# A fused attention and two-layer MLP kernel: the split of layer 2's input goes to GpSimd, one weight conversion for all, other orders at the start and the end

## The chip, the cores and the metric

One Trainium2 chip, one core. The metric is the device time of one execution in microseconds (us). The kernel before was run three times: 1339.81, 1341.20 and 1343.64 us, median 1341.2 us.

## The reference, cut to what matters

```python
# q (1,12288,128), kv (1,384,32,128), w_sr (128,128): float32; the four MLP weights come as float64
kv_pool = kv.reshape(B, H // 4, 4, W // 4, 4, C).mean(axis=(2, 4))     # 12288 rows -> 768 keys
k = v = kv_pool.reshape(B, -1, C) @ w_sr
a = softmax(q @ k.T / sqrt(128));  x = a @ v                            # 12288 x 128
h = x @ w_in;   x2 = (h * clip(h + 3, 0, 6) / 6) @ w_out                # layer 1, 128 -> 2048 -> 128
h = x2 @ w_in2; g = where(h >= 1, h, where(h <= -1, 0, (h + 1)**2 / 4))
out = g @ w_out2                                                        # layer 2, 128 -> 2048 -> 128
```

## The kernel before, in words

The 12288 queries are worked on in 24 blocks of 512. All products are made from two 16-bit parts of each factor, a high part (the value rounded) and a low part (the value minus the high part): three matmuls stand for one. So every activation is split before TensorE can use it: ScalarE rounds (`x_hi` L681, `cast` L785, `a_hi` L652), and VectorE or GpSimd subtracts (`x_lo` L687, `a_lo` L657, `low` L791, the last on GpSimd).

**Slots.** A block has 8 slots; slot T does 256 of the 2048 inner columns of layer 1 for pair s = T, and of layer 2 for pair s = T - 11 (`O2` L21). There are 192 pairs and 11 slots more at the end, in which layer 2 runs alone. In a slot TensorE does two times three matmuls of `m_in` (L695) and six of `m_out` (L710) for each layer. Attention of a later block is spread over the slots: four score tiles (`s`, `n`, `e`, `t`, `u`, `w`), two products with the values (`v`), the transpose of the queries (`q`, with its split in `i` and `j`).

**Orders written by hand.** `PROLOGUE` (L28) is the order of everything before slot 0: maxima of the weights (`m`), pooling of the keys (`k`, `g`, `t`), their product with w_sr (`p`, `z`, `y`), conversion of weights (`j`), attention of block 0, the first queries of block 1. Then `slot(T)` (L890) walks through one list of steps in each slot: `RAMP` (L38) in the slots before `RAMP_T` = 22, `SLOT` (L40) from there on. `name:g` means that the step is done g slots late. Each engine runs its instructions in the order in which these lists issue them. `LOADS` (L26) is the order of the input DMAs; a load is issued when one of 16 staging buffers has come free. They go through SyncE's queue, as do the transposes of the attention weights (L663) and the output DMAs (L741).

**Layer 2's input.** When layer 1 of a block is complete, its sum lies in a PSUM bank. `x2_max` (D, L490, VectorE) takes the largest magnitude in each partition, `x2_copy` (R, L496, ScalarE) copies the bank to SBUF, `x2_sum` (P, L499, TensorE) adds over partitions, `x2_scales` (F, L506 to L511, VectorE) makes a power of two of it and eight scalars, `x2_hi` (G, L516, ScalarE) and `x2_lo` (H, L521, VectorE) split. The first matmul of layer 2 for the block (step A0) needs both parts. F stands in slot 1 of the eight (counted from the block's end), G and H in slot 2, A0 in slot 3. The query transpose `q` stands in slot 2 as well.

**Weights.** They arrive as float64 and are turned into float32 bits with integer operations. For layer 1's input weight (4 tiles) this takes four stages (`w_stage0` to `w_stage3`, L291 to L336) on ScalarE, VectorE and GpSimd; for the other 12 tiles three (`w_new0`, `w_new1`, `w_stage3`). The largest magnitude of the first goes over GpSimd (`w_top_pool`, L208), of the other three over TensorE (`w_top_row`, `w_top_all`, L215 to L221). Seven tiles are converted in the prologue, nine in the slots of `CONV_AT` (steps B0, B1, B2).

**Keys.** Each of the 12 key tiles is pooled in one of three modes (`KV_MODE` L27): P, 16 matmuls into 32 of the partitions, then a copy and a TensorE transpose per pair of tiles; D, 16 matmuls with the tile as the weights, which need no transpose; V, two additions on VectorE and a few matmuls.

**The end.** Layer 2's sum of a block lies in the bank `acc1` until `o_T` (T, L734) has transposed it; `o_scale` (U, L739, ScalarE) scales it, four DMAs store it. The next block's first `m_out` of layer 2 waits for that bank.

Of the kernel before, what the change touches and what calls it, by code (L numbers as in the profile page):

```python
# [19 lines left out]
W_MIN = 3.4332275390625e-05  # L20
# [39 lines left out]
def tile_attn_moe_moe2(  # L60
# [70 lines left out]
    def new_h():  # L131
        return ps_h.tile([128, 512], FP32, tag="h", name="h")
# [18 lines left out]
    late = [0 if f"j{n}.{2 + (n % 2 == 0)}" in PROLOGUE.split() else 1 for n in range(len(late))]  # L151
# [55 lines left out]
    def w_top_pool(n):
        nc.gpsimd.partition_all_reduce(mw[n][:, 1:2], mw[n][:, 0:1], channels=128,  # L208
                                       reduce_op=bass_isa.ReduceOp.max)
        w_tops[n] = mw[n][:, 1:2]  # L210
# [13 lines left out]


    def w_scales(n):
        sc, u, v = w_sc[n], w_sc[n].bitcast(U32), mw[n].bitcast(U32)
        nc.vector.tensor_scalar(out=mw[n][:, 0:1], in0=w_tops[n], scalar1=2.0 ** -14, scalar2=None,
                                op0=ALU.max)
        nc.vector.tensor_scalar(out=v[:, 2:3], in0=v[:, 0:1], scalar1=0x7F800000, scalar2=None,  # L230
                                op0=ALU.bitwise_and)
# [59 lines left out]
    def w_stage0(job):  # L291
        t = wst[job][0]
        m, which, i = job
        half = W_DT[m] == FP16
        sc = w_sc[2 * m + (which == "out")]
        a = wk_p.tile([128, WP], U32, tag="wa", name="wa")
        r = wk_p.tile([128, WP], I32, tag="wr", name="wr")
        nc.scalar.activation(out=a.bitcast(FP32), in_=t[:, :, 1].bitcast(FP32), func=ACTF.Abs,
                             scale=sc[:, 0:1] if half else 1.0)
        low = t.rearrange("p a b -> p (a b)").bitcast(U8).rearrange("p (a b) -> p a b", b=8)  # L300
        if half:
            nc.scalar.activation(out=r.bitcast(FP32), in_=low[:, :, 3], func=ACTF.Identity,
                                 scale=sc[:, 2:3], bias=sc[:, 1:2])
        else:
            nc.scalar.activation(
                out=r, in_=low[:, :, 3], func=ACTF.Copy, scale=1.0 / 32.0, bias=1.0 / 64.0
            )
        wcv[job] = (a, r)

    def w_stage1(job):  # L310
        a, r = wcv[job]
# [4 lines left out]
        nc.gpsimd.tensor_tensor(out=a.bitcast(I32), in0=a.bitcast(I32), in1=r, op=ALU.add)

    def w_stage2(job):
        a, r = wcv.pop(job)
        hi32 = wst[job][0][:, :, 1]  # L320
        keep = 0x80000000 if W_DT[job[0]] == FP16 else 0xC0000000
        nc.vector.scalar_tensor_tensor(out=hi32, in0=hi32, scalar=keep, in1=a,
                                       op0=ALU.bitwise_and, op1=ALU.bitwise_or)

    def w_stage3(job):
# [7 lines left out]
        (nc.gpsimd.tensor_copy if w_new(job) and job not in LO_DVE else nc.scalar.copy)(out=hi[:, sl], in_=w)  # L333
# [39 lines left out]
    def kv_pool(i):  # L373
        m, mode = i // 2, KV_MODE[i]
        t = kv_t[i][0]
# [5 lines left out]
        for g in range(2):  # L381
# [9 lines left out]
        if mode == "P" and i % 2 == 1:  # L391
            nc.scalar.copy(out=pk[:, m * 128:(m + 1) * 128], in_=ps[:, :128])
# [597 lines left out]
```

## Time and profile before

| | |
|---|---|
| runs of the kernel before | 1339.81, 1341.20, 1343.64 us; median 1341.2 |
| the profiled execution | 1342.52 us; its span, first to last instruction, 1340.7 us |
| busy share of the span | TensorE 93%, VectorE 89%, ScalarE 86%, GpSimd 70% |
| chain that ended last | TensorE 59%, VectorE 20%, ScalarE 11% |

PE is TensorE's matmuls, PEld its weight loads, DVE VectorE, ACT ScalarE, POOL GpSimd, SP SyncE. Matmuls are pipelined: one of 512 columns is shown with 379 ns, while the next starts some 216 ns after it. "Idle before" is the time in which an engine did nothing just before an instruction, and "<-" names what ended it, inferred from semaphore events.

### The profile page before, as it was taken

The numbers are of one execution on the slowest core, as the hardware profiler recorded it, in microseconds if no ns is written. First come the engines' busy times: TensorE is split into PE (matmuls) and PEld (weight loads), VectorE is DVE, ScalarE is ACT, GpSimd is POOL, SyncE is SP. The second block draws the span as 40 slices with busy tenths as digits, with TensorE's granted clock in tenths as the row PEclk, the third lists the DMA queues.
The fourth block names the chain that finished last, engine by engine and source line by source line (L and its number), as shares of the span: only waits on it lengthen the run. The fifth ranks groups of instructions, "written<-read, shape, count | busy, mean of one in ns | idle before, by whom it ended". The sixth has DMA issues, their size and how long they took to land.

```text
span 1340.7 us, 19138 instructions
## 1 busy us (share of the span) xinstructions
PE 1247.0 (93%) x6280; PEld 662.2 (49%) x6280; DVE 1187.5 (89%) x1944; ACT 1158.6 (86%) x2028; POOL 941.9 (70%) x825
## 2 busy tenths in 40 slices
PE   7466789999999999999999999999999999999996
PEld 6333445455455555555455555555555555555442
DVE  4676799999999999999999999999999999999887
ACT  3465788998999998999998998899999999999986
POOL 2244687777777777777777777777777777777874
PEclk9687899999999999999999999999999999999998
DMA  8821113222222212222122122222122121121000
GB/s 301 219 44 36 32 26 50 44 39 45 39 37 53 40 35 52 36 40 52 32 44 52 33 44 49 33 46 47 36 45 44 37 48 36 32 45 32 1 9 17
DMA packets 260788, 66.32 MB, mean 49 GB/s; under 512 B 252368, under 2 KB 256592, under 8 KB 260688
## 3 DMA queue, kind: packets, MB, share of 16 engines
q1 hardware_dynamic: 257888, 63.73, 23.8%
q10 hardware_dynamic: 2800, 1.38, 0.4%
q8 instruction: 49, 0.80, 0.2%
q14 instruction: 51, 0.42, 0.1%
HBM read 21.04 MB, written 6.29 MB: 20 GB/s over the span
## 4 chain that ended last, share of the span: by engine, by line
PE 59%; DVE 20%; ACT 11%; issue 1%; DVEq 0%; ACTq 0%
PE h L707 24%; PE acc L725 23%; PE s L673 6%; PE s L593 5%; DVE g L777 5%; ACT h L785 4%; DVE g L764 3%; ACT t L749 2%; DVE t L756 2%; DVE x2l L521 2%; DVE bs L511 2%; ACT g L772 2%; ACT a L652 2%; DVE nm L604 2%; DVE bs L510 1%
## 5 line engine op out<-in xcount | busy, mean ns | idle before, releaser
L791 POOL TENSOR_TENSOR l<-g,h 128x512 f16<-128x512 f32 x382 | 450.1, 1196 | 274.7 <-DVE a L657 135.0
L791 POOL TENSOR_TENSOR l<-t,h 128x512 f16<-128x512 f32 x382 | 438.6, 1170 | 42.2 <-ACT h L785 39.2
L764 DVE TENSOR_SCALAR g<-h,bs 128x512 f32<-128x512 f32 x384 | 292.7, 804 | 23.7 <-PE h L707 23.6
L756 DVE SCALAR_TENSOR_TENSOR t<-t,h 128x512 f32<-128x512 f32 x384 | 255.8, 682 | 29.1 <-ACT t L749 25.9
L777 DVE SCALAR_TENSOR_TENSOR g<-g,bs,h 128x512 f32<-128x512 f32 x384 | 267.9, 737 | 14.0 <-ACT g L772 13.2
L785 ACT CAST h<-g 128x512 f16<-128x512 f32 x384 | 235.1, 615 | 42.2 <-PE acc L725 40.2
L749 ACT ACTIVATE t<-h,h_sc 128x512 f32<-128x512 f32 x384 | 252.5, 676 | 21.1 <-PE h L707 21.0
L772 ACT ACTIVATE g<-g,bs 128x512 f32<-128x512 f32 x384 | 259.7, 717 | 6.8 <-DVE g L764 3.6
L785 ACT CAST h<-t 128x512 f16<-128x512 f32 x384 | 235.6, 618 | 22.6 <-DVE t L756 21.2
L707 PE MATMUL h<-x2h,wi1h 128*128 128x512 f16 x384 | 145.6, 379 | 16.8 <-DVE g L777 16.8
L707 PE MATMUL h<-xh,wi0h 128*128 128x512 f16 x384 | 146.8, 382 | 10.2 <-ACT xh L681 6.2
L725 PE MATMUL acc<-h,wo1h 128*128 128x512 f16 x384 | 146.0, 380 | 3.9 <-DVE o L734 3.8
L725 PE MATMUL acc<-l,wo1h 128*128 128x512 f16 x384 | 145.9, 380 | 1.5 <-POOL l L791 1.5
L725 PE MATMUL acc<-h,wo0h 128*128 128x512 f16 x384 | 146.5, 381 | 0.8 <-DVE bs L506 0.8
L725 PE MATMUL acc<-l,wo0h 128*128 128x512 f16 x384 | 146.3, 381 | 0.5 <-DVE l L791 0.5
L725 PE MATMUL acc<-h,wo0l 128*128 128x512 f16 x384 | 146.1, 380 | 0.0
L725 PE MATMUL acc<-h,wo1l 128*128 128x512 f16 x384 | 146.0, 380 | 0.0
L707 PE MATMUL h<-xl,wi0h 128*128 128x512 f16 x384 | 145.9, 380 | 0.1
L707 PE MATMUL h<-xh,wi0l 128*128 128x512 f16 x384 | 146.0, 380 | 0.0
L707 PE MATMUL h<-x2h,wi1l 128*128 128x512 f16 x384 | 145.7, 379 | 0.0
L707 PE MATMUL h<-x2l,wi1h 128*128 128x512 f16 x384 | 145.5, 379 | 0.0
L707 PEld LDWEIGHTS <-wi1h 128*128 128x128 f16 x768 | 75.1, 98 | 113.9 <-issue 26.9
(183 smaller groups left out, 1843.6 us busy)
## 6 DMA issues: line engine op xcount, KB each, us to landing
out_dram<-o SPq DMA_DIRECT2D x96, 64.0 KB, 1.9
q<-in_q_dram SPq DMA_DIRECT2D x92, 64.0 KB, 2.3
wst<-in_kv_dram SPq DMA_DIRECT2D x9, 512.0 KB, 7.5
wst<-in_moe_w_in_dram SPq DMA_DIRECT2D x6, 512.0 KB, 6.2
wst<-in_moe_w_out_dram SPq DMA_DIRECT2D x5, 512.0 KB, 4.8
at<-a SPq DMA_TRANSPOSE x96, 3.7
g<-in_moe_w_out_dram SPq DMA_DIRECT2D x2, 512.0 KB, 7.9
g<-in_moe_w_in_dram SPq DMA_DIRECT2D x1, 512.0 KB, 4.2
```

What stands on the lines that cost most here:

```text
L511: nc.vector.tensor_scalar(out=t[:, 8:10], in0=b_k[:, 3:5], scalar1=t[:, 3:4], scalar2=None, op0=ALU.mult)
L593: nc.tensor.matmul(ps[h], l[:, js], r[:, ks], start=(n == 0), stop=(n == 2))
L673: nc.tensor.matmul(ps, l[:, k, :], r[:, k, :], start=(n == 0), stop=(n == 3 * KC - 1))
L707: nc.tensor.matmul(ps, l[:, ws], r, start=(n == 0), stop=(n == 2))
L725: nc.tensor.matmul(acc[m], l[:, ws], r[:, k, :], start=(c == 0 and i == 0), stop=(c == NPAIR - 1 and i == 5))
L749: nc.scalar.activation(out=g_t[0, s][:, k], in_=h_t[0, s, k], func=ACTF.Relu, scale=h_sc, bias=0.5 * H_SC)
L756: nc.vector.scalar_tensor_tensor(out=g, in0=g, scalar=H_SC, in1=h_t.pop((0, s, k)), op0=ALU.min, op1=ALU.mult)
L764: nc.vector.tensor_scalar(out=g_t[1, s][:, k], in0=h_t[1, s, k], scalar1=bs_t[s // NPAIR][:, 6:7], scalar2=bs_t[s // NPAIR][:, 7:8], op0=A ...
L772: nc.scalar.activation(out=g, in_=g, func=ACTF.Square, scale=bs_t[s // NPAIR][:, 8:9], bias=0.5)
L777: nc.vector.scalar_tensor_tensor(out=g, in0=g, scalar=bs_t[s // NPAIR][:, 6:7], in1=h_t.pop((1, s, k)), op0=ALU.mult, op1=ALU.max)
L785: nc.scalar.copy(out=hl_t[m, s][0][:, k], in_=g_t[m, s][:, k])
L791: eng.tensor_tensor(out=lo[:, k], in0=g_t[m, s][:, k], in1=hi[:, k], op=ALU.subtract)
```

## The change

- `x2_scales` keeps three instructions on VectorE; the two that make eight scalars go to GpSimd, into `x2_hi`. `x2_hi` scales the copy in place on GpSimd, `x2_lo` casts and subtracts on GpSimd. Five GpSimd instructions a block stand for three of VectorE and ScalarE.
- `q_hi` goes from ScalarE to GpSimd for blocks 2 and later, `o_scale` from ScalarE to GpSimd (VectorE in the last block).
- All 16 weight tiles are converted by the three stages. Layer 1's input weight has a power-of-two scale of its own for that (`x_scale`), taken into `x_sc`. Its largest magnitude goes over TensorE (`it`, `ib`).
- The V mode of the keys isn't used; P alternates between the two groups of a tile.
- `PROLOGUE`, `LOADS`, `RAMP` and `SLOT` are new orders, `RAMP` ends at slot 18, and the slots from 192 on have an order of their own, `TAIL`.
- In the last 11 slots every second pair of layer 2 takes score banks and layer 1's buffers, and the last block's layer 2 sums in `acc0`.

```diff
-LOADS = "w k0 k1 q0 w w w k2 k4 k3 k6 k5 k8 k7 k9 k10 k11 w w w w q1 w w w w w q2 w w w"
-KV_MODE = "DDVVPPPPPPPP"
+LOADS = "w k1 k3 k0 k2 w w w k4 k6 w k5 k7 w k8 k9 q0 k10 w w q1 k11 w w w w w q2 w w w"
+KV_MODE = "PPDDPPPPPPDD"
 PROLOGUE = """
...
-N3 e3 a2 b1 vs a3 vh b2 b3 vl m5 m7 oa ot q1 ob oc hs j1.0 x0 j1.1 j3.0 x1 j3.1 j1.2 j5.0 j3.2
-j5.1 j5.2
+k1 k2 g1 m0 m6 m4 m2 ia g3 it ib ic g2 g4 j2.0 k6 k4 j0.0 j2.1 k5 k3 g0 g5 k0 t1 p1 t2 g7 k7 p2 z1
...
+N2 vs n3 b0 e2 a2 N3 a1 oa e3 b2 ot vh b1 ob a3 q1 oc j5.0 b3 vl j1.0 j5.1 j1.1 j5.2 j3.0 j3.1 x0 x1
+j3.2 hs j1.2
 """
-RAMP_T = 22
-RAMP = """a0:0 r0:0 a1:0 r1:0 t:1 u:1 m0:0 m1:0 D:1 R:1 G:2 H:2 x:0 A0:0 K0:0 A1:0 K1:0 C0:1 L0:1 C1:1 L1:1 c0:0 l0:0 c1:0 l1:0
-T:3 U:3 Q0:0 Q1:0 s:0 n:0 w:1 P:1 F:1 X0:0 X1:0 e:0 v:0 z:0 y:0 q:0 i:0 j:0 B1:1 B2:2 B0:0 f o:1 O:2"""
+RAMP_T = 18
+RAMP = """
+a0 l0:1 j:2 q:1 L1:2 r0 a1 o:2 X1:1 x e:1 r1 f:1 y:1 O:3 m0 A0 G:2 A1 B0:1 l1:1 T:3 H:2 R:1 U:4 s D:1
+P:1 t:1 C0:1 m1 K0 K1 v F:1 C1:1 n c0 Q0 B1:1 L0:1 u:1 B2:3 z c1 X0 w:1 i:1 Q1
+"""
 SLOT = """
-a0 r0 B2:3 o:2 a1 l1:1 u:1 O:3 G:2 r1 y:1 D:1 B0:2 C0:1 R:1 m0 A0 A1 v w:1 c0 H:2 C1:1 j:1 m1 c1 K0
-K1 Q0 P:1 T:3 L0:1 s n q F:1 Q1 B1:3 L1:1 X0 e X1 f:1 t U:3 i z l0
+a0 L1:2 X1:1 t:1 r0 u:1 l0:1 o:2 z:1 a1 D:1 O:3 r1 A0 A1 q l1:1 G:2 y:1 v m0 w:1 C0:1 m1 R:1 T:3 i
+C1:1 c0 K0 K1 P:1 f:1 s j:1 U:3 c1 Q0 n B0:2 Q1 F:1 L0:1 H:2 B2:2 X0 B1:4 e
 """
+TAIL = """
+B2:3 n:1 P:2 L0:2 Q1:1 F:2 a0 B0:3 c0 m1:1 o:2 a1 O:3 D:1 c1 w:1 l0:1 s e r1 z:1 L1:2 v A0 t:1 T:3
+R:1 X0:1 G:2 i q j:1 l1:1 u:1 B1:4 X1:1 y:1 K0 C0:1 C1:1 r0 m0 A1 K1 U:3 H:2 Q0 f:1
+"""
+TAIL_T = 192
...
 def x2_scales(b):
...
-        nc.vector.tensor_scalar(out=t[:, 5:8], in0=b_k[:, 0:3], scalar1=t[:, 4:5], scalar2=None, op0=ALU.mult)
-        nc.vector.tensor_scalar(out=t[:, 8:10], in0=b_k[:, 3:5], scalar1=t[:, 3:4], scalar2=None, op0=ALU.mult)
 def x2_hi(b):
...
-        nc.scalar.activation(out=x2_t[b][0], in_=xr_t[b], func=ACTF.Copy, scale=bs_t[b][:, 5:6])
+        nc.gpsimd.tensor_scalar(out=t[:, 5:8], in0=b_k[:, 0:3], scalar1=t[:, 4:5], scalar2=None, op0=ALU.mult)
+        nc.gpsimd.tensor_scalar(out=t[:, 8:10], in0=b_k[:, 3:5], scalar1=t[:, 3:4], scalar2=None, op0=ALU.mult)
+        nc.gpsimd.tensor_scalar(out=xr, in0=xr, scalar1=t[:, 5:6], scalar2=None, op0=ALU.mult)
 def x2_lo(b):
...
-        nc.vector.scalar_tensor_tensor(
-            out=lo, in0=xr_t.pop(b), scalar=bs_t[b][:, 5:6], in1=hi, op0=ALU.mult, op1=ALU.subtract
-        )
+        xr = xr_t.pop(b)
+        nc.gpsimd.tensor_copy(out=hi, in_=xr)
+        nc.gpsimd.tensor_tensor(out=lo, in0=xr, in1=hi, op=ALU.subtract)
 def q_hi(b):
...
-        nc.scalar.copy(out=hi, in_=t)
+        (nc.gpsimd.tensor_copy if b > 1 else nc.scalar.copy)(out=hi, in_=t)
 def o_scale(b):
...
-        nc.scalar.activation(out=o, in_=o, func=ACTF.Copy, scale=bs_t[b][:, 9:10])
+        (nc.vector if b == NB - 1 else nc.gpsimd).tensor_scalar(out=o, in0=o, scalar1=bs_t[b][:, 9:10], scalar2=None, op0=ALU.mult)
...
+def spare(s):
+        return s > NS - O2 and (NS - s) % 2 == 0
 def m_in(m, s, k):
...
+        if m and spare(s):
+            if k == 0:
+                tail_s[s] = new_s()
+            ps = tail_s[s][:, k]
+        else:
+            ps = new_h()
 def m_out(m, s):
...
-            acc[m] = ps_a.tile([128, BLK], FP32, tag=f"acc{m}", name=f"acc{m}")
+            bank = "acc0" if b == NB - 1 else f"acc{m}"
+            acc[m] = ps_a.tile([128, BLK], FP32, tag=bank, name=bank)
```

## Rows read from the trace of the kernel before

**Rows 1.** Stages of core 0: length, busy us of each engine (instructions), granted clock, DMA share, GB/s.

```profile
0.00:71.45 71.45, 43.29 (x280) 34.70 (x280) 41.29 (x105) 28.00 (x58) 17.78 (x21) 0.86 0.80 244
71.45:203.10 131.65, 92.58 (x433) 51.12 (x434) 103.74 (x183) 92.21 (x161) 78.66 (x69) 0.88 0.21 37
203.10:290.50 87.40, 85.42 (x429) 44.56 (x428) 80.24 (x127) 80.98 (x143) 65.44 (x57) 1.00 0.27 44
290.50:1201.60 911.10, 900.70 (x4556) 473.78 (x4554) 843.93 (x1351) 843.00 (x1478) 681.21 (x595) 1.00 0.23 42
...
1291.50:1340.70 49.20, 35.51 (x152) 14.84 (x150) 39.35 (x58) 32.81 (x50) 25.97 (x22) 0.93 0.07 11
```

**Rows 2.** TensorE's waits, 290.5 to 1201.6 us: total, times, longest.

```profile
PE h L707 <- DVE g L777: 9.2, 27, 0.5
```

**Rows 3.** Timeline of VectorE: start, duration; `x2_max` of three blocks in a row.

```profile
1056.78 0.67 DVE L490 TENSOR_REDUCE mb<-acc 128x1 bf16<-128x512 f32 x1
...
1106.90 0.67 DVE L490 TENSOR_REDUCE mb<-acc 128x1 bf16<-128x512 f32 x1
...
1158.02 0.67 DVE L490 TENSOR_REDUCE mb<-acc 128x1 bf16<-128x512 f32 x1
```

**Rows 4.** The chain in order of time, pieces on `x2_lo`: start, us.

```profile
306.46 1.73 DVE x2l L521
...
1116.26 1.73 DVE x2l L521
```

**Rows 5.** Instructions on the tiles bs and x2l: min/median/max ns, first and last start.

```profile
L510 DVE TENSOR_SCALAR bs<-b_k,bs x24: 478/764/942, 139.9 to 1299.7; 128x3 f32<-128x3 f32 x24
L511 DVE TENSOR_SCALAR bs<-b_k,bs x24: 215/1198/1203, 140.7 to 1300.1; 128x2 f32<-128x2 f32 x24
...
L521 DVE SCALAR_TENSOR_TENSOR x2l<-xr,bs,x2h x24: 736/744/1733, 148.1 to 1301.5; 128x512 f16<-128x512 f32 x24
```

**Rows 6.** Groups by form, 290.5 to 1201.6 us: busy, mean ns, idle before, releasers.

```profile
L657 DVE SCALAR_TENSOR_TENSOR a<-e,rc,a 128x768 f16<-128x768 f32 x72 | 73.2, 1017 | 17.7 <-ACT a L652 15.8 <-DMA q<-in_q_dram 1.9
...
L516 ACT ACTIVATE x2h<-xr,bs 128x512 f16<-128x512 f32 x18 | 13.0, 725 | 0.0
...
L565 ACT CAST qh<-qT 128x512 fp32r<-128x512 f32 x18 | 10.9, 607 | 0.0
...
L791 POOL TENSOR_TENSOR l<-g,h 128x512 f16<-128x512 f32 x288 | 337.0, 1188 | 217.4 <-DVE a L657 124.5 <-ACT h L785 88.1 <-DVE t L756 2.5
```

**Rows 7.** Casts and subtractions of weight tiles on GpSimd (L333, L336): min/median/max ns.

```profile
L333 POOL CAST wo0h<-t x1: 634/634/634, 66.4 to 66.4; 128x512 f16<-128x512 f32 x1
L333 POOL CAST wo0h<-g x1: 1035/1035/1035, 69.3 to 69.3; 128x512 f16<-128x512 f32 x1
...
L336 POOL TENSOR_TENSOR wo0l<-t,wo0h x1: 1500/1500/1500, 67.2 to 67.2; 128x512 f16<-128x512 f32 x1
```

**Rows 8.** Timeline of one block: F's third instruction, and A0's first matmul.

```profile
605.91 0.17 DVE L509 RECIPROCAL bs<-bs 128x1 f32<-128x1 f32 x1
...
615.46 0.38 PE L707 MATMUL h<-x2h,wi1h 128*128 128x512 f16 x1
```

**Rows 9.** Timelines of TensorE and ScalarE, 0 to 80 us; in brackets the idle time before.

```profile
7.27 3.59 PE L387 MATMUL h<-pool_m,g 128*128 128x32 f32 x16 [7.27 <-DMA g<-in_kv_dram]
...
32.12 2.46 PE L385 MATMUL h<-wst,pool_m 128*32 128x128 f32 x32
...
60.43 0.61 PE L673 MATMUL h<-at,vh 128*128 128x256 f16 x2
...
70.90 0.65 ACT L333 CAST wo0h<-g 128x512 f16<-128x512 f32 x1 [3.12 <-DVE g L288]
71.45 1.26 ACT L749 ACTIVATE t<-h,h_sc 128x512 f32<-128x512 f32 x2
```

**Rows 10.** Timelines of TensorE and VectorE at the end.

```profile
1313.32 0.61 PE L725 MATMUL acc<-h,wo1h 128*128 128x512 f16 x1 [3.79 <-DVE o L734]
...
1317.08 1.53 DVE L764 TENSOR_SCALAR g<-h,bs 128x512 f32<-128x512 f32 x2 [2.52 <-PE h L707]
```

More of the change, by code (lines that the diff above doesn't have):

```diff
@@ L150, in tile_attn_moe_moe2 @@
     late = [0] * sum(f"j{j}.0" in PROLOGUE.split() for j in range(16))
-    late = [0 if f"j{n}.{2 + (n % 2 == 0)}" in PROLOGUE.split() else 1 for n in range(len(late))]
+    late = [0 if f"j{n}.2" in PROLOGUE.split() else 1 for n in range(len(late))]
     late += [1 if t + 3 < O2 else 2 for t in CONV_AT]
@@ L204, in w_top @@
     def w_top(n):
+        step("top", n)
+        for i in range(4):
+            assert ("max", (n, i)) in did
         nc.vector.tensor_reduce(out=mw[n][:, 0:1], in_=mw[n], axis=AX.X, op=ALU.max)
[L207 to L210, printed above, removed]
     def w_top_row(n):
-        step("row", n)
+        step("row", n, "top")
         w_tops[n] = new_h()
@@ L332, in w_stage3 @@
         sl = slice(i * WP, (i + 1) * WP)
-        (nc.gpsimd.tensor_copy if w_new(job) and job not in LO_DVE else nc.scalar.copy)(out=hi[:, sl], in_=w)
+        (nc.gpsimd.tensor_copy if job not in LO_DVE else nc.scalar.copy)(out=hi[:, sl], in_=w)
         eng = nc.vector if job in LO_DVE else nc.gpsimd
@@ L380, in kv_pool @@
         ps = pool_ps(m)
-        for g in range(2):
-            p0 = (2 * (i % 2) + g) * 32
+        if mode == "P":
             for j in range(4):
-                if mode == "P":
+                for g in range(2):
+                    p0 = (2 * (i % 2) + g) * 32
                     nc.tensor.matmul(ps[p0:p0 + 32, :128], pool_m, t[:, g, j], start=(j == 0), stop=(j == 3))
-                else:
+        else:
+            for g in range(2):
+                p0 = (2 * (i % 2) + g) * 32
+                for j in range(4):
                     nc.tensor.matmul(
@@ L390, in kv_pool @@
         died(kv_t[i][1])
-        if mode == "P" and i % 2 == 1:
+        if mode == "P" and ("k", i ^ 1) in did:
             nc.scalar.copy(out=pk[:, m * 128:(m + 1) * 128], in_=ps[:, :128])
     def kv_sum_mm(i):
+        if KV_MODE[i] != "V":
+            return
         t, rec = kv_t[i]
+        step("g", i, "k")
         ps = pool_ps(i // 2)
@@ L402, in kv_poolT @@
     def kv_poolT(m):
+        for i in (2 * m, 2 * m + 1):
+            assert ("g" if KV_MODE[i] == "V" else "k", i) in did
         ms = slice(m * 128, (m + 1) * 128)
@@ L428, in v_scale @@
     def v_scale():
+        for m in range(KC):
+            assert ("y", m) in did
         nc.vector.tensor_reduce(out=mx[:, 0:1], in_=mx, axis=AX.X, op=ALU.max)
@@ L680, in x_hi @@
         hi, lo = (t[:, i * 256:(i + 1) * 256] for t in x_t[b])
-        nc.scalar.activation(out=hi, in_=x_ps[b, i], func=ACTF.Copy, scale=2.0 ** -13)
+        nc.scalar.activation(out=hi, in_=x_ps[b, i], func=ACTF.Copy, scale=x_sc)
     def x_lo(b, i):
@@ L885, in tile_attn_moe_moe2 @@
     early_of = {bi: T < O2 for T, bi in av_at.items()}
[L886 removed]
+    orders = [[(n, int(g or 0)) for n, _, g in (t.partition(":") for t in o.split())] for o in (RAMP, SLOT, TAIL)]
     served = {}
     def slot(T):
[L891 removed]
+        for n, g in orders[(T >= RAMP_T) + (T >= TAIL_T)]:
             at, f = ops[n]
```

111 lines of the change are left out of this document (36 added, 75 removed).

## The prediction

> **What bounds the kernel now.** I read first the stages [rows 1]; they begin at the first ReLU of slots 0, 18, 32 and 176, and the last of them some 4 us after slot 191's ReLU. The middle, 290.5 to 1201.6, is 18 blocks in 911.10 us, 50.62 a block, and holds two thirds of the time. There TensorE is busy 900.70 us, so 10.4 us are left to win from waits alone. VectorE (843.93) and ScalarE (843.00) are at 93% each, GpSimd (681.21) at 75%. Second, TensorE's waits in that stretch [rows 2]: 9.2 us of its 10.4 idle us end with VectorE's `max2`, which gives back a PSUM bank of layer 2. Third, where VectorE is late: `x2_max` comes once a block, and the blocks have two lengths, 50.12 and 51.12 us [rows 3]. The chain of waits shows a piece of 1.73 us on `x2_lo` in each long block [rows 4]: nine in the 18 blocks, of which the first and the last are shown, and the last, at 1116.26, lies in the long block of [rows 3]. In the others this instruction takes its median of 0.74 us [rows 5]. One us late on VectorE at this place is one us of the block. The two small instructions before it behave likewise, 1.20 us for 128x2 elements where the shortest takes 0.215 [rows 5]. At the end GpSimd idles, where 1.20 was the rule and 0.215 the exception; so I read all three as VectorE held up while GpSimd works on SBUF.
>
> The other losses are outside the middle. Slots 0 to 17 take 131.65 us, 7.31 a slot, the next 14 take 87.40, or 6.24. In the former no engine is full: VectorE 103.74 of 131.65 (79%), ScalarE 92.21, TensorE 92.58 at a granted clock of 0.88. The last 49.20 us have VectorE at 39.35, TensorE at 35.51.
>
> **The change, part by part.**
>
> *VectorE and ScalarE in a block.* VectorE loses 0.76 + 1.20 + 0.74 or 1.73 [rows 5], on average 3.2 of its 46.9 us a block (843.93 / 18). ScalarE loses 0.725 (`x2_hi`), 0.607 (`q_hi`) [rows 6] and `o_scale`, which has the shape of `x2_hi` and which I put at the same 0.7: 2.0 of 46.8. Both were beside TensorE's work, so the removed time as such is worth nothing; worth something is the lateness. With `x2_lo` gone from VectorE the long blocks should become short: 9 x 1.00 = 9.0 us. If all of TensorE's idle time goes, it is 10.4. Below, nothing is won if another wait takes its place. I take 10, because VectorE also loses the two small instructions right before it. What would be late next is TensorE's own sequence.
>
> *GpSimd in a block.* Added are seven instructions. Casts on GpSimd took 0.634 to 1.035 us [rows 7], subtractions 1.188 on average [rows 6] to 1.50 [rows 7]. A multiplication by a scalar isn't in the trace; it lies between a cast (one input) and the slowest subtraction (two), 0.63 to 1.50, and I take 0.8, near the cast, since it reads one tensor. The two small ones have no row on GpSimd; VectorE's give 0.2 to 1.2 each, and I take 0.4. So the split costs 0.8 + 0.8 + 0.63 + 1.19 = 3.4 us (2.9 to 6.4), and with the queries' cast (0.63) and the output's scale (0.8) GpSimd goes from 37.8 (681.21 / 18) to 42.7 us a block, 47 at the upper ends. That is under 50.1, so it isn't a bound; and 217.4 us of idle time stand in front of its subtractions [rows 6], 12 a block, which hide it.
>
> The Trainium skill (GPSIMD Engine Reference, section 4.1) speaks against this move: elementwise work belongs on VectorE, GpSimd being about twice as slow with two inputs. The rows agree in direction (1.188 on GpSimd, 0.74 on VectorE), and by that rule the split would lose; it doesn't look at which engine has time left.
>
> *The path of the split.* F's third instruction ends at 605.91 + 0.17 = 606.08, A0's first matmul of the block starts at 615.46 [rows 8]: 9.38 us. GpSimd has in this stretch at most the four subtractions of a slot (4 x 1.19 = 4.75) and the queries' cast (0.63), which the new order puts between G and H. That leaves 4.0 us for the split at 3.4. Some of the subtractions ahead of G will have run before F ends, so I cost it at nothing; the cover ends at 4.0.
>
> *SyncE's queue.* The four output DMAs now wait for GpSimd's `o_scale`, and behind them in the queue stand the transposes of `a`. U is in slot 5 of the eight, after GpSimd's slot 2 with the split, and GpSimd has its 12 idle us to reach it; nothing. The new order moves `a_lo`, B0 to B2 and the lows by less than a slot; they are used a slot or more later: nothing.
>
> *Before slot 0 (71.45 us).* Three edits. The last keys are loaded behind eight weight tiles instead of four, and behind q1: 4 x 0.52 + 0.26 = 2.4 MB at the stage's 244 GB/s [rows 1] is 10 us. The last two key tiles go by mode D, 3.59 us each, where both took 2.46 by P [rows 9]: 5 us. Against that, the same bytes stand in the queues in all (DMA share 0.80), and the first product with the values, at 60.43, came 20 us after the scores because the transposes queue with the weights; so part of the 15 us is hidden there. And slot 0's first ReLU at 71.45 stood behind a cast of a weight tile at 70.90 which had waited 3.12 us for VectorE [rows 9]; in the new order those conversions come before x1, some 3.5 us won. The removed V additions, the fourth conversion stage and the maximum over GpSimd lie in the first 45 us, in which VectorE is at 41.29 and ScalarE at 28.00 of 71.45: nothing. Sum 0, from -4 to +10.
>
> *Slots 0 to 17.* `RAMP` of before issues every step of a slot in the slot itself; the new one puts subtractions, casts and `a_hi` a slot late, as `SLOT` does. At best VectorE gets as full as in the next stage: 80.24 / 87.40 = 92%, and 103.74 less 5 (two splits) over 0.92 is 107, 24 us won. At worst nothing is won: the waits may be those of the transposes and of the weights. I take a third, 8.
>
> *The end.* TensorE waits 3.79 us for `o_T`, and VectorE then idles 2.52 for the matmuls [rows 10]; with `acc0` that goes: 2.5. VectorE, the busiest there, also loses 0.48 + 0.22 + 0.74 = 1.4 [rows 5]. But for block 23 the split is on the path, and GpSimd's 3.4 stand for 0.725 + 1.4 = 2.2: back 1.2. Sum 2.7, call it 3; from -7 (most of VectorE's 9.9 idle us but the output's) to +3 (split at 6.4).
>
> **The sum.** -10 - 0 - 8 - 3 = -21. The profiled execution took 1342.5, its span 1340.7; that gives 1321.5. The median of the runs is 1.3 lower, so 1320.
>
> **The rivals.**
>
> *A: the ends are worth more.* `RAMP` gets 24 instead of 8, the end 7 instead of 3: -41, 1300. For it: nothing is full there. Against: the transposes and weights arrive when they do. Chance 0.13.
>
> *B: the start eats it.* The keys come 10 us later and the ramp gains nothing: -10 + 10 - 3, plus the 3.5 not won with it at most: about 1336 to 1340. For it: the loads' order; against: the 20 us between scores and values. Chance 0.12.
>
> *C: the split comes late.* Above 4.0 us on GpSimd A0 waits. At 5.0 it is 1 us a block in 22 blocks, +22, which cancels everything: 1342. For it: the upper ends; against: the subtractions of that slot rarely all stand in the stretch. Chance 0.08.
>
> *D: `a_lo` gets stuck behind GpSimd (slower).* `a_lo` reads two SBUF tensors like `x2_lo`. Now it takes 1.017 on average, hence is never held, and 124.5 us of GpSimd's idle time end with it [rows 6]: GpSimd stands still while it runs. With GpSimd at 85% and in another order, each of four a block may be held for up to a subtraction, 1.2. From one unhidden us a block on (22 of 21 us won) it decides; with two it is +44 - 21, 1364. Against: VectorE has 3.2 us more to absorb it. Chance 0.12. The Trainium skill has this as a rule (SBUF — State Buffer, "Who interferes with whom"): the pair of ports is locked for a whole instruction, a VectorE instruction with two SBUF inputs contends with a GpSimd one that reads SBUF, and whoever starts first wins. By that rule rows 5 are explained, and D depends on the order alone.
>
> *E: the change doesn't make the blocks even.* The 1.73 comes from something else and stays as a wait for `max2`: -11, 1330; within my own range.
>
> **Chances and range.** The forecast (with E) 0.55, 1310 to 1331; A 0.13, B 0.12, C 0.08, D 0.12. A difference under 0.3% (4 us) can't be told from none here. Faster: forecast, A, and nearly all of B, 0.79; same: most of C and a rest of B, 0.08; slower: D and a bit of C, 0.13. The range leaves out D and the half of A below 1303: 1303 to 1341.
>
> **What would show it.** Right: all blocks of the middle at 50.1 or less, `max2` gone from TensorE's waits, GpSimd at 42 to 44 us a block, its two small instructions near 0.4 and the scaling near 0.8, `a_lo` still near 1.02. Wrong: A0 waiting for a GpSimd subtraction (C); `a_lo` at two lengths (D); slot 0's first ReLU after 75 us (B); slots 0 to 17 still at 130 us. The forecast is wrong as a whole if the middle stays above 50.4 a block.

## The result, and the profile after

The kernel after takes 1290.03 us (median of four runs, 1286.86 to 1291.47), the kernel before beside it 1340.51; the ratio is 0.9621, interval [0.959, 0.9651]. The forecast was 1320, with a range from 1303 to 1341: the sign is right, the gain is 50 us instead of 21, and the time lies below the range. The profiled execution took 1290.69 us, its span 1288.9.

The stages of after, cut at the same events as [rows 1] (length, busy time and instructions of PE, PEld, DVE, ACT and POOL, granted clock, DMA share, GB/s):

```profile
0.00:65.66 65.66, 42.08 (x293) 33.80 (x294) 35.38 (x97) 24.85 (x55) 14.24 (x20) 0.84 0.87 265
65.66:167.64 101.98, 91.42 (x443) 50.31 (x442) 93.39 (x177) 89.38 (x157) 82.64 (x75) 0.93 0.24 45
167.64:253.88 86.24, 85.93 (x434) 45.10 (x432) 79.53 (x125) 79.09 (x138) 78.67 (x72) 1.00 0.30 49
253.88:1148.12 894.24, 894.24 (x4555) 473.80 (x4554) 818.84 (x1297) 816.71 (x1423) 789.27 (x721) 1.00 0.25 43
...
1238.10:1288.90 50.80, 35.79 (x152) 14.99 (x150) 37.89 (x56) 30.96 (x47) 30.38 (x28) 0.95 0.06 11
```

From first ReLU to first ReLU, against before (us):

| stage | before | after | difference | forecast |
|---|---|---|---|---|
| before slot 0 | 71.45 | 65.66 | -5.8 | 0 |
| slots 0 to 17 | 131.6 | 102.0 | -29.6 | -8 |
| slots 18 to 31 | 87.5 | 86.2 | -1.2 | with the middle |
| slots 32 to 175, 18 blocks | 911.0 | 894.2 | -16.8 | -10 |
| slots 176 to 190 | 84.4 | 84.4 | 0 | with the middle |
| from slot 191's ReLU to the end | 54.8 | 56.4 | +1.6 | -3 |

More than half of the gain is in slots 0 to 17, where no engine was full; there VectorE goes from 79% to 92% busy (93.39 of 101.98) and TensorE from 70% to 90%. In the middle TensorE is shown busy for the whole 894.24 us, with no wait, and sixteen of the eighteen runs below have the same length to 0.01 us (all but e1 and e4), so it is read as the least that TensorE needs there; the `max2` of [rows 2] is gone, and `x2_max` comes every 49.7 us (three in 99.4 us). The same one-line view of `x2_max` as it stands in after (count, shortest/median/longest ns, first and last start):

```profile
L463 DVE TENSOR_REDUCE mb<-acc x3: 674/674/674, 260.4 to 359.8; 128x1 bf16<-128x512 f32 x3
```

What GpSimd now does in the middle, by shape, against [rows 6 and 7] (count, then busy us, mean ns, then idle before and what ended it):

```profile
L778 POOL TENSOR_TENSOR l<-t,h 128x512 f16<-128x512 f32 x289 | 329.5, 1163 | 0.0
L778 POOL TENSOR_TENSOR l<-g,h 128x512 f16<-128x512 f32 x288 | 329.4, 1163 | 65.0 <-DVE a L631 54.8 <-ACT h L772 10.2
L545 POOL TENSOR_TENSOR ql<-qT,qh 128x512 fp32r<-128x512 f32 x18 | 35.8, 1991 | 0.0
L490 POOL TENSOR_SCALAR xr<-xr,bs 128x512 f32<-128x512 f32 x18 | 28.3, 1571 | 0.0
L725 POOL TENSOR_SCALAR o<-o,bs 128x512 f32<-128x512 f32 x18 | 28.2, 1568 | 38.5 <-DVE o L720 38.5
L497 POOL TENSOR_TENSOR x2l<-xr,x2h 128x512 f16<-128x512 f32 x18 | 20.9, 1158 | 1.4
L496 POOL CAST x2h<-xr 128x512 f16<-128x512 f32 x18 | 11.1, 615 | 0.0
L539 POOL CAST qh<-qT 128x512 fp32r<-128x512 f32 x18 | 11.0, 613 | 0.0
L488 POOL TENSOR_SCALAR bs<-b_k,bs 128x3 f32<-128x3 f32 x18 | 5.6, 313 | 0.0
L489 POOL TENSOR_SCALAR bs<-b_k,bs 128x2 f32<-128x2 f32 x18 | 5.4, 302 | 0.0
```

The split costs 0.31 + 0.30 + 1.57 + 0.62 + 1.16 = 3.96 us a block; GpSimd's whole work is 43.8 a block (789.27 / 18).

### The profile page after: what moved, and what is told of

Read it like the earlier page. It is cut to its first block, busy times and chain, and to the rows that moved or that the text cites. A ratio compares the mean times of both kernels' runs of the same rounds, so it can differ in the third digit from the quotient of the medians.

```text
span 1288.9 us, 19053 instructions
## 1 busy us (share of the span) xinstructions
PE 1239.0 (96%) x6307; PEld 661.2 (51%) x6307; DVE 1140.4 (88%) x1865; ACT 1120.2 (87%) x1954; POOL 1078.3 (84%) x989
## 4 chain that ended last, share of the span: by engine, by line
PE 86%; DVE 7%; ACT 2%; DMA 2%; issue 1%; POOL 1%; SPq 0%; DVEq 0%; ACTq 0%
PE acc L711 35%; PE h L692 35%; PE s L567 7%; PE s L647 6%; DVE g L764 1%; DVE g L751 1%; DVE a L631 1%; DVE t L742 1%; DMA wst<-in_moe_w_in_dram 1%; PE h L647 1%; ACT h L772 1%; DMA wst<-in_kv_dram 1%; PE h L347 1%; DVE t L751 0%; PE h L352 0%
## 5 line engine op out<-in xcount | busy, mean ns | idle before, releaser
L778 POOL TENSOR_TENSOR l<-g,h 128x512 f16<-128x512 f32 x372 | 427.7, 1169 | 82.7 <-DVE a L631 61.1
L778 POOL TENSOR_TENSOR l<-t,h 128x512 f16<-128x512 f32 x392 | 452.8, 1176 | 21.1 <-ACT h L772 21.1
L751 DVE TENSOR_SCALAR g<-h,bs 128x512 f32<-128x512 f32 x374 | 284.4, 801 | 36.2 <-PE h L692 34.3
L759 ACT ACTIVATE g<-g,bs 128x512 f32<-128x512 f32 x374 | 255.2, 717 | 18.2 <-DVE g L751 15.4
L772 ACT CAST h<-g 128x512 f16<-128x512 f32 x374 | 214.6, 615 | 44.2 <-PE acc L711 41.5
L772 ACT CAST h<-t 128x512 f16<-128x512 f32 x394 | 228.2, 617 | 19.5 <-DVE t L742 15.0
L692 PE MATMUL h<-x2h,wi1h 128*128 128x512 f16 x374 | 142.1, 380 | 2.6 <-DVE g L764 2.6
L692 PE MATMUL h<-x2l,wi1h 128*128 128x512 f16 x374 | 142.1, 380 | 0.0
L692 PE MATMUL h<-x2h,wi1l 128*128 128x512 f16 x374 | 142.1, 380 | 0.0
L631 DVE SCALAR_TENSOR_TENSOR a<-e,rc,a 128x768 f16<-128x768 f32 x96 | 124.5, 1297 | 18.3 <-ACT a L626 18.1
```

Source lines behind the costliest of these rows:

```text
L631: nc.vector.scalar_tensor_tensor(out=a[:, 1], in0=e, scalar=rc, in1=a[:, 0], op0=ALU.mult, op1=ALU.subtract)
L692: nc.tensor.matmul(ps, l[:, ws], r, start=(n == 0), stop=(n == 2))
L751: nc.vector.tensor_scalar(out=g_t[1, s][:, k], in0=h_t[1, s, k], scalar1=bs_t[s // NPAIR][:, 6:7], scalar2=bs_t[s // NPAIR][:, 7:8], op0=A ...
L759: nc.scalar.activation(out=g, in_=g, func=ACTF.Square, scale=bs_t[s // NPAIR][:, 8:9], bias=0.5)
L772: nc.scalar.copy(out=hl_t[m, s][0][:, k], in_=g_t[m, s][:, k])
L778: eng.tensor_tensor(out=lo[:, k], in0=g_t[m, s][:, k], in1=hi[:, k], op=ALU.subtract)
```

## The experiments

Line numbers are those of each kernel. "Stretch" is slots 0 to 17, "block" the usual distance of two `x2_max` in the middle (in before the mean of its two lengths, 50.62), "start" the first ReLU, "end" the time from slot 191's ReLU on; all are read from the one profiled execution of a run. The chips differ: the kernel before took 1340 to 1355 us beside these runs, so lengths of stages are compared rather than totals wherever runs come from different chips. Profiles of the same code differ: the start of after was seen between 63.0 and 66.6, its stretch between 101.3 and 103.1 (after, e5, e8, e15, e18), and its end between 54.7 and 57.9 (the thirteen profiles with the same code there).

### The middle: split or order?

**e1**: the kernel after, with `x2_scales`, `x2_hi` and `x2_lo` of before.

> The changed kernel with the split of layer 2's input back where it was: eight scalars and x2_lo on VectorE, x2_hi on ScalarE; all orders, the queries' cast and the output's scale stay as changed. Theory 1 (the orders made the slots 0 to 17 short, the move of the split made the blocks even): the middle's blocks go from 49.68 back to 50.1 to 51.1 us, slots 0 to 17 stay at 102 us (+-3), in all 1298 to 1316. Theory 2 (relief of VectorE made both short): slots 0 to 17 go to 108 us or more as well, in all over 1316. Theory 3 (the new SLOT order alone evens the blocks, wherever the split is done): blocks stay at 49.7 to 49.8, in all under 1294.

Measured: 1296.83 us, blocks 49.90, stretch 102.3, start 65.1.

**e2**: the kernel before, with only the three functions of after.

> The kernel before with only the split of layer 2's input moved to GpSimd (two small instructions, scale in place, cast, subtraction), all orders as before. Theory 1: the long blocks go, 50.62 becomes 49.7 to 50.1, so 9 to 17 us less in the middle; slots 0 to 17 lose only what two splits cost VectorE, 131.6 to 126 or more; in all 1318 to 1332. Theory 2: slots 0 to 17 fall to 115 or less, in all under 1315. Theory 3: the blocks stay at 50.6 or get longer, because in the old order the subtractions of GpSimd are then late; in all 1335 or more.

Measured: 1326.30 us, blocks 49.68, stretch 134.0.

**e4**: the kernel before, with only the list `SLOT` of after.

> The kernel before with only the new SLOT order (from slot 22 on), split on VectorE and ScalarE. Theory 1: VectorE's small instructions and x2_lo still meet GpSimd, the blocks stay at 50.1 to 51.1 on average 50.4 or more; in all 1335 to 1345. Theory 3: blocks of 49.7 to 49.9, in all 1322 to 1330.

Measured: 1327.49 us, blocks 49.87, stretch 131.6.

Each of the two alone makes the blocks even: the split 50.62 - 49.68 = 0.94 us a block, the order 0.75, both together 0.94. They remove the same lateness. With the new order the split is worth only 0.22 a block, though VectorE still does these instructions in e1. VectorE's `bs` and `x2l` in e4 over the whole run (count, busy us, mean ns):

```profile
L511 DVE TENSOR_SCALAR bs<-b_k,bs 128x2 f32<-128x2 f32 x24 | 27.8, 1159 | 0.0
L521 DVE SCALAR_TENSOR_TENSOR x2l<-xr,bs,x2h 128x512 f16<-128x512 f32 x24 | 22.0, 917 | 0.0
```

The hold-up of the small instruction is as long as in [rows 5]. That of `x2_lo` is mostly gone: in the middle it takes 0.85 us on average, against 1.23 in before. What is left no longer falls where TensorE needs VectorE: TensorE's waits in the middle of e4 come to 0.3 us, against 9.2 in [rows 2]. None of the three shortens the stretch beyond its kernel's own (102.0 and 131.6).

### Slots 0 to 17: one step or the whole order?

**e3**: the kernel after, with the slots' first order and its tables (`RAMP`, `RAMP_T`, `EARLY`, `CONV_AT`, `MX`, `SPLIT_AT`) of before.

> The changed kernel with the old RAMP order up to slot 22 and the tables that go with it (when attention of blocks 1 and 2, the weight conversions and the weights' maxima come). Theory 1: slots 0 to 17 go from 102 back to 122 to 132 us, the middle stays at 49.68 a block; in all 1310 to 1321. Theory 2: they stay under 112, in all under 1300.

Measured: 1322.04 us, stretch 134.4, blocks 49.68. The lists alone are worth 32 us. TensorE's granted clock in the stretch isn't what they win: e3 had 0.89 and after 0.93, but e11 below also had 0.93 and took 125.1, and e8 had 1.00 and took 101.3. What waited there, in before (71.45 to 203.1) and then in after (65.66 to 167.64): engine and tile, what it waited for, us, times, longest.

```profile
POOL l L791 <- ACT h L785: 45.0, 14, 6.2
...
DVE t L756 <- ACT t L749: 16.1, 13, 1.9
ACT e L633 <- DVE nm L604: 12.9, 8, 5.1
...
PE h L215 <- DVE mw L205: 10.6, 2, 8.3
```

```profile
POOL l L778 <- ACT h L772: 17.3, 15, 3.0
...
PE h L226 <- DVE wtop L225: 2.6, 2, 1.7
...
DVE t L742 <- ACT t L735: 0.2, 1, 0.2
```

So theories were made of single waits: the exponential, the maxima, the conversions.

**e7**: e3, the exponential behind the next slot's ReLUs.

```diff
-RAMP: ... a1:0 r1:0 t:1 ... X1:0 e:0 v:0 ...
+RAMP: ... a1:0 r1:0 e:1 t:1 ... X1:0 v:0 ...
```

> The run with the old RAMP order, with one step moved: the exponential (e) goes from the end of a slot to behind the two ReLUs of the next slot. Theory 1a (in the old RAMP ScalarE waits at the end of the slot for VectorE's maximum, and then VectorE for the ReLU behind it, 17 us of waits of the product behind the ReLU): slots 0 to 17 go from 134 to 112 to 124 us, in all 1300 to 1312. Theory 1b (it is the whole order: casts, subtractions and the products each in their own slot): 130 us or more, in all over 1317.

Measured: 1327.76 us, stretch 139.7, 5 us longer. The wait only changes its owner; this one, 2.1 us in before and in e3, is the second longest in e7:

```profile
DVE su L614 <- ACT e L605: 22.4, 11, 3.4
```

**e9**: after, with only the table `MX` (when the maxima are taken) of before. **e11**: e3 with the `MX` of after (one conversion comes a slot later, since its scale is known later).

> The changed kernel with the old table of when layer 2's weight maxima are taken: the transpose of a maximum and the step that answers it stand in the same slot again (slots 2 and 5), so that TensorE's queue waits for VectorE. Theory 1c (of the 32 us of the slots 0 to 17 a third is this wait: 10.6 us in the trace before, 2.6 after): slots 0 to 17 go from 102 to 108 to 114 us, in all 1296 to 1302. Theory 1b (the order of the steps within a slot does it): 101 to 105, in all 1288 to 1293.

> The run with the old RAMP order (1322.0), with the new table of the weight maxima (one conversion comes a slot later, since its scale is known later). Theory 1c: slots 0 to 17 go from 134 to 122 to 128 us, in all 1309 to 1316. Theory 1b: 131 or more, in all 1318 to 1326.

Measured: e9 1289.81 us, stretch 101.7; e11 1310.22, stretch 125.1. The maxima are worth 9 us in the old order and nothing in the new one. e11 shows a pattern, slot after slot (timeline: start, duration, idle before):

```profile
114.98 0.69 DVE L285 SCALAR_TENSOR_TENSOR g<-g,acc 128x512 uint32<-128x512 uint32 x1
115.70 0.74 ACT L275 ACTIVATE acc<-g,ws 128x512 f32<-128x512 f32 x1 [1.88 <-DVE g L285]
116.38 0.66 ACT L277 ACTIVATE wr<-g 128x512 int32<-128x512 uint8 x1
116.94 1.26 ACT L733 ACTIVATE t<-h,h_sc 128x512 f32<-128x512 f32 x2
117.65 1.28 DVE L740 SCALAR_TENSOR_TENSOR t<-t,h 128x512 f32<-128x512 f32 x2 [1.98 <-ACT t L733]
```

VectorE's part of a weight conversion ends, ScalarE's part of the next one starts, the ReLUs stand behind it, and VectorE's product waits 1.98 us for them. The next theory was the place of the conversion.

**e13**: e11, ScalarE's part (`B0`) moved to the middle of the slot. **e14**: after with `MX` and `CONV_AT` of before and all three parts at the slot's end.

```diff
-e13 RAMP: ... m1:0 D:1 ...      ... B1:1 B2:2 B0:0 f ...
+e13 RAMP: ... m1:0 B0:1 D:1 ... ... B1:1 B2:2 f ...
-e14 RAMP: ... A1 B0:1 l1:1 ... Q0 B1:1 L0:1 u:1 B2:3 z ... i:1 Q1
+e14 RAMP: ... A1 l1:1 ...      Q0 L0:1 u:1 z ...      i:1 Q1 B1:1 B2:2 B0:0
```

> The run with the old RAMP order and the new maxima times (1310.2), with one step moved: the first stage of a weight conversion (B0, two ScalarE instructions) goes from the end of its slot to behind the two products of the next one. Theory 1d (its result lies in the one free PSUM bank; at the end of the slot it waits for VectorE to be done with the previous tile in that bank, the next slot's two ReLUs stand behind it, and VectorE waits some 1.7 to 2.0 us for them in nine slots): slots 0 to 17 go from 125 to 107 to 116 us, in all 1292 to 1301. Rival (the ping-pong is spread over all steps of the slot): 120 us or more, in all over 1304.

> The reverse: the changed kernel with the old times of maxima and conversions, and the three conversion steps at the end of the slot as in the old RAMP (B1, B2, B0 behind the last step). With the old maxima alone slots 0 to 17 took 101.7 us. Theory 1d: 110 to 120, in all 1296 to 1308. Rival: 101 to 106, in all 1287 to 1293.

Measured: e13 1305.88 us (1302.13 and 1309.63), stretch 123.3, read from the slower of the two; e14 1304.05, stretch 116.8. The two executions of e13 lie 7.5 us apart, so how little the move wins is not sure. In e13 the product's wait halves (16.1 in e11), and another, 4.8 in e11, doubles:

```profile
ACT t L733 <- PE h L690: 9.3, 6, 1.9
DVE t L740 <- ACT t L733: 8.8, 9, 2.3
```

**e10**: after, with `SLOT` (plus the steps of the start) from slot 0 on. **e12**: after, the subtractions `l0`, `l1` in their own slot.

> The changed kernel with the SLOT order in the slots 0 to 17 too, with the weight conversions and maxima put at the places they have in RAMP. Theory 1b (any order in which products, casts, subtractions and exponentials stand a slot behind their matmuls keeps the engines apart): 100 to 110 us for slots 0 to 17, in all 1287 to 1297. Rival (the RAMP order is particular, made for slots without layer 2): 115 us or more, in all over 1302.

> The changed kernel with layer 1's subtraction on GpSimd back in the slot of its cast (l0 and l1 directly behind the second cast) in slots 0 to 17; the output matmuls stay two slots late. Theory 1b in its narrow form (GpSimd's queue, which in the old order waits 42 us for casts, is what the lag frees): slots 0 to 17 go to 107 or more, in all over 1294. Rival (GpSimd isn't on the path of the ramp, the lag of VectorE's and ScalarE's steps is): 100 to 104, in all 1287 to 1292.

Measured: e10 1302.45 us, stretch 115.7; e12 1293.62, stretch 105.0. So steps that lag a slot are not enough by themselves: `SLOT`, which has them too, costs 14 us here, and the subtractions alone 3.

Do these prices add? **e16**: e11 with all three parts of the conversion where the new order has them. **e17**: e14 with the subtractions in their own slot as well. **e18**: after, unchanged, on their chip.

> The old order of slots 0 to 17 with the new times of the maxima (125.1 us for the stretch), and now all three steps of a weight conversion where the new order has them: the first in the middle of the slot, the second and third between layer 2's products, the third one slot later. If the conversion's place is worth by itself the 15 us that it was worth in the new order, the stretch takes about 110 us. If in the old order every slot is a chain of several steps that wait for each other, and the conversion only one of them, it stays at 120 us or more.

> The new order of slots 0 to 17 with three groups of steps put back at once: the conversions at the slot's end and the old times of the maxima (116.8 us together), and the subtractions in their own slot (worth 3 us alone). If the prices add, the stretch takes about 120 us, and the other 14 of the old order's 134 belong to the steps that still stand late in it. If these steps are what holds the old order back, it takes 128 us or more.

> The kernel after, unchanged, on the chip of the two others: slots 0 to 17 at 102 us. If they take over 104, the stretches of different chips can't be compared to within 2 us.

Measured: e16 1313.91 us, stretch 128.7; e17 1304.26, stretch 116.9; e18 1290.57, stretch 101.3. They don't add. The conversion at the slot's end, with the old times of conversions and maxima, costs the new order 15 us (the maxima alone nothing, e9); the subtractions on top of that nothing; and the conversion's new place gains the old order nothing (128.7 against 125.1). None of the steps tried carries the 32 us. In the old order ScalarE and VectorE wait for each other at several places of each slot, and e7 and e13 show a moved wait come back at another place; that this explains the whole is argued from such lists and not shown. The 17 us between 116.9 and 134.4 were not taken apart further: the times of attention (`EARLY`, `SPLIT_AT`) and the end of `RAMP` were never changed alone.

### The start

**e6**: after, with `PROLOGUE`, `LOADS` and `KV_MODE` of before (conversion stays short).

> The changed kernel with the old order before slot 0: old PROLOGUE, LOADS and key modes (VectorE additions for two key tiles included); conversions and everything from slot 0 on as changed. Theory 1 (the 6 us before slot 0 come from these orders): slot 0's first ReLU goes from 65.7 back to 70 to 73 us and the end follows, in all 1294 to 1299. Rival (they come from the shorter conversion of the four tiles and the maximum over TensorE): it stays at 64 to 67, in all 1288 to 1292.

Measured: 1295.35 us, start 68.2. Timeline of e6 at the first ReLU, then of after (compare [rows 9]):

```profile
67.67 0.65 ACT L298 CAST wo0h<-g 128x512 f16<-128x512 f32 x1 [3.17 <-DVE g L287]
68.22 1.26 ACT L735 ACTIVATE t<-h,h_sc 128x512 f32<-128x512 f32 x2
```

```profile
57.91 0.59 PE L647 MATMUL h<-at,vh 128*128 128x256 f16 x2 [3.95 <-DMA at<-a]
...
65.66 1.34 ACT L735 ACTIVATE t<-h,h_sc 128x512 f32<-128x512 f32 x2 [1.20 <-PE h L692]
```

With the old lists the ReLU again stands behind a cast that waits for VectorE; in after it stands behind TensorE. The other 3 us (71.45 to 68.2) came with the old lists too, so from the shorter conversion or from the new way of the maximum. The maximum isn't it: ScalarE's first step with the scale starts at 17.04 in e6 and already at 16.17 in before. The conversion acts on SyncE's queue, whose load waits for a free staging buffer. The load's issue and the queue's wait in front of it, in before and then in e6:

```profile
18.48 12.68 SPq L183 DMA_DIRECT2D g<-in_moe_w_out_dram  x2
...
SPq L183 <- POOL wi0l L336: 9.8, 1, 9.8
```

```profile
18.19 9.13 SPq L189 DMA_DIRECT2D g<-in_moe_w_out_dram  x2
...
SPq L189 <- POOL wi0l L301: 6.3, 1, 6.3
```

The wait for the conversion's last step is 3.5 us shorter, the transposes behind the loads begin at 43.61 instead of 47.30, and the first product with the values starts at 56.39 instead of 60.43. That the one leads to the other is read from the queue and wasn't tried by itself.

### The end

The last stretch took 56.4 us instead of 54.8. That difference alone is within what the profiles of one code differ by (54.7 to 57.9); what stands out is a wait that before doesn't have. TensorE's waits in the last 51 us of after:

```profile
PE s L692 <- DVE t L751: 7.3, 5, 2.2
PE s L692 <- POOL x2l L497: 0.9, 1, 0.9
```

And one of the five (timeline):

```profile
1266.90 0.81 DVE L751 TENSOR_SCALAR t<-s,bs 128x512 f32<-128x512 f32 x1
1267.76 0.38 PE L692 MATMUL s<-x2h,wi1h 128*128 128x512 f16 x1 [1.36 <-DVE t L751]
...
1268.61 0.81 DVE L751 TENSOR_SCALAR t<-s,bs 128x512 f32<-128x512 f32 x1 [0.90 <-PE s L692]
```

Every second pair takes score tile `s`, whose two banks are one tile. VectorE's clip (K0) reads the first half; `A1` writes the other half and is issued behind K0 in `TAIL`, so it waits for it, and the second clip waits for `A1`. Two kernels take this away in two ways: **e5** issues `A1` directly behind `A0`; **e8** lets the second pairs keep their old banks.

```diff
-e5 TAIL: ... v A0 t:1 ... r0 m0 A1 K1 U:3 ...
+e5 TAIL: ... v A0 A1 t:1 ... r0 m0 K1 U:3 ...
+e8 spare(): return False
```

> The changed kernel with one step moved in TAIL: A1 directly behind A0, ahead of VectorE's clip of the pair's first half. The trace of the changed kernel shows the second half's matmuls of every second pair wait 1.4 to 2.2 us for that clip (7.3 us in five waits), because both halves lie in one score tile. Theory 1 (this false dependence makes the end 1.5 us longer than before): the end, from slot 191's ReLU on, goes from 56.4 to 50 to 53 us, in all 1284 to 1287. Rival (VectorE is full there anyway, or the split of block 23 on GpSimd sets the end): it stays at 55.5 or more, in all 1289 to 1291.

> The changed kernel without the spare buffers: all pairs of layer 2 take the ordinary banks and buffers at the end; TAIL and acc0 stay. Theory 1 (the score tile shared by two halves costs the end some 5 us): the end goes from 56.4 to 50 to 54 us, in all 1284 to 1288. Rival (the spare buffers help, the TAIL order or GpSimd's split cost): the end is 56 or more, in all 1290 to 1296.

Measured: e5 1284.71 us (four runs, 1284.22 to 1286.95), ratio to before 0.955 [0.9525, 0.9574], end 50.7; e8 1284.63, end 51.8. In e5 TensorE's longest waits are these; that for `t` is gone:

```profile
PE acc L711 <- POOL l L778: 1.9, 5, 0.9
PE s L692 <- POOL x2h L496: 1.1, 1, 1.1
```

The two ends lie below all thirteen of the old code. e5 is faster than both kernels, and its interval doesn't meet that of after.

**e15**: e5 with the old `LOADS`, to see whether the loads' order costs what was forecast.

> The changed kernel with A1 behind A0 in TAIL (1284.7 alone) and the old order of the loads, in which the last keys come before four more weight tiles; stages tell the two apart. If the later keys cost time before slot 0, as the prediction's rival B had it, slot 0's first ReLU goes from 65 to 60 to 63 us, in all 1280 to 1283. If they are hidden or the weights of layer 1's output then come too late, it stays at 64.5 or goes up to 70, in all 1284 to 1290.

Measured: 1289.15 us, ratio 0.9616 [0.9576, 0.9655], start 69.3, end 50.9. The new loads' order gains some 4 us, in the total (1289.15 against 1284.71) as in the start (69.3 against 64.9). In e15 three weight loads stand in the queue right ahead of the transposes, and the first product with the values comes 4.2 us later than in e5. The queue and that product, in e15 and then in e5:

```profile
47.95 2.22 SPq L189 DMA_DIRECT2D wst<-in_moe_w_out_dram  x3
50.26 8.49 SPq L637 DMA_TRANSPOSE at<-a  x3
...
61.39 0.59 PE L647 MATMUL h<-at,vh 128*128 128x256 f16 x2 [6.79 <-ACT wr L279]
```

```profile
48.62 6.03 SPq L637 DMA_TRANSPOSE at<-a  x3
...
57.16 0.59 PE L647 MATMUL h<-at,vh 128*128 128x256 f16 x2 [3.95 <-DMA at<-a]
```

In both the product follows the end of the third transpose's issue by 2.5 to 2.6 us (58.75 and 54.65). In e15 the view puts the end of the wait down to a step of ScalarE that ended at the same time, so that the transposes are the cause is read from the order and not shown.

## Why the prediction was right or wrong

*The middle: mechanism right, size low (-10 forecast, -16.8).* Lateness of VectorE in the middle was the loss, and it went. Two things were off. The floor, "TensorE is busy 900.70 us, so 10.4 us are left", was too high: the same matmuls (4556 and 4555 of them) take 894.24 in after. A matmul of 512 columns is shown with 379 ns while the next starts 216 ns later, so a gap of up to 0.16 us behind it is shown as busy; 6.5 us of waiting stood inside the busy time. e4 says the same: blocks 0.19 longer than e2's, with one wait of 0.3 us in all 18. And the gain was put down to the split alone: e4 shows that the order by itself does nearly as much, so whoever had priced the two parts one by one would have counted the same lateness twice.

*GpSimd's price: total near, parts not.* 43.8 us a block against 42.7; with the scaling at twice its forecast, that is partly luck. The scaling was put "near the cast, since it reads one tensor", at 0.8; it took 1.57, more than the upper end of 1.50, and so did the output's scale (1.57). The cast (0.62) and the subtraction (1.16) came out as costed, the small ones a little lower (0.30 each instead of 0.4). The split took 3.96 us, where the cover was put at 4.0. It had more: in after VectorE's part ends at 613.48, GpSimd starts at 615.00 and ends at 620.62, and the block's first matmul starts at 622.87, 9.39 us behind VectorE's part (9.38 before), 2.25 to spare. The queries' cast and one of the subtractions stood between the split's own instructions and were covered too. Rival C didn't come.

*Rival D: seen, and hidden.* `a_lo` in the middle of after (shortest, median, longest ns):

```profile
L631 DVE SCALAR_TENSOR_TENSOR a<-e,rc,a x72: 1009/1102/2042, 261.6 to 1144.4; 128x768 f16<-128x768 f32 x72
```

Its mean is 1312 against 1017 [rows 6]: 72 x 0.295 = 21 us of VectorE's time. TensorE waits for none of it; VectorE had lost 3.2 us a block and paid back 1.2. The step on which D was put below the forecast, VectorE's slack, held. That D "depends on the order alone" did not hold: with the new `SLOT` but the split on VectorE no `a_lo` is held (1.02 us at most in e4, mean 1.017 in e1 too), with the split alone it takes 1.146 on average (e2). In e4 (the same window of 18 blocks):

```profile
L657 DVE SCALAR_TENSOR_TENSOR a<-e,rc,a x72: 1010/1018/1020, 297.3 to 1183.7; 128x768 f16<-128x768 f32 x72
```

The trace agrees with the rule of the Trainium skill that was cited there (SBUF — State Buffer, "Who interferes with whom"): the holding up moved with the split from `x2_lo` (mean 1.23 in the middle of before) to `a_lo` (1.312). The other rule of the Trainium skill that was cited, that elementwise work belongs on VectorE (GPSIMD Engine Reference, section 4.1), gave the wrong sign here: 1.16 on GpSimd against 0.74 on VectorE, and still e2 gains 0.94 us a block.

*Slots 0 to 17: the step that failed (-8 forecast, -30).* "At best VectorE gets as full as in the next stage ... I take a third" took a third of a bound that was nearly right itself: 24 at best, 29.6 measured, at just the 92% that was named. The rest is VectorE's own work, which fell by 10.35 us where 5 had been taken off: the split is 4.2 of it (99.50 in e2), and with the new order and the split on VectorE it is also down, at 93.90 (e1). The doubt was that the waits "may be those of the transposes and of the weights". The list of waits of that stretch would have settled it: none of its rows is on a DMA; the longest is GpSimd's wait for ScalarE's cast, 45.0 us. Rival A had the 24, and was given 0.13.

*The start: 0 forecast, -6.* The 3.5 us for the cast ahead of the ReLU were right in kind (e6). Three steps failed. The loads' order was costed at up to 10 us and gains about 4 (e15). The shorter conversion was put at "nothing" because VectorE and ScalarE had room; some 3 us came with it (e6), and what the profile shows for it is a wait in the loads' queue that is 3.5 us shorter. And the two late key tiles weren't seen as a loss: the first product with the values came 2.5 us sooner, though no run changes their mode alone. Each of the single prices has the scatter of the start around it, 63.0 to 66.6.

*The end: -3 forecast, +1.6, which the scatter of the end doesn't tell from none.* The shared tile wasn't looked at; "with `acc0` that goes" dealt with a wait that was there and did go, not with the one that the new order brings (7.3 us). e5 shows the end without it: 50.7, that is -4.1 against before, near the forecast.

The errors sum up: -21.6 (slots 0 to 17), -5.8 (start), -6.8 (middle), +4.6 (end) and -1.2 (slots 18 to 31) give -30.8, the distance between the -21 of the forecast and the -51.8 between the two profiled spans.

Two slips in the working change nothing: rival B's -10 + 10 - 3, with up to 3.5 more, comes to 1338 to 1342 and not to 1336 to 1340, and the last stage of [rows 1] begins 5.6 us after slot 191's ReLU, not 4.

## What to carry to other kernels

Where no engine is full, look at the list of waits before taking a fraction of the best case: if the waits are between two compute engines and not on DMAs, a new order can bring the stretch near the next engine's limit. Here it did so as a whole; single moves in the old order won from -5 to 9 us of 32. When two parts of a change cure the same lateness, price them together. When two halves of one tile are written and read in turn, check in which order they are issued: in this kernel a write to one half waited for the read of the other.

## What the runs showed of the hardware that was not expected

- On GpSimd, multiplying 128x512 f32 in place by one scalar per partition takes 1571 ns, longer than subtracting two tensors (1158) and 2.5 times a cast to f16 (615).
- GpSimd's `ql` (two inputs, 128x512, to fp32r) takes 1991 ns on average in the middle of after, its other subtractions 1163; in before the same step took 1274. It too goes with the split: 1272 in e1, 1996 in e2. What holds it wasn't looked into.
- TensorE's busy time as shown isn't a floor: it was 900.70 us in the middle of before and 894.24 in after, and e4's blocks are 0.19 us longer than e2's with 0.3 us of waits shown in 18 blocks.
- VectorE's `a_lo`, never over 1.02 us in the middle while VectorE did the split (before, e1, e4), takes up to 2.04 us in after, where GpSimd does it.
